# A new hand-written order for the first five units of a state-space scan feeding a squared-ReLU feed-forward, with w_in and w_out quarters issued earlier

## The chip, the cores and the metric

The kernel runs on one core of a Trainium2 chip. The metric is the device time of one execution in microseconds (us), less being better. The page of the profile shows one execution; its span runs from the first to the last instruction of the program.

The engines have short names in the profile. PE is TensorE, and PEld its weight loads. DVE (VectorE), ACT (ScalarE) and POOL (GpSimd) do the elementwise work. SP (SyncE) issues transfers, as ACT and POOL can.

## The reference

A chunked state-space scan over 4 batches and 8 heads, 768 positions, head width 32 and state width 16, is followed by a feed-forward with a squared ReLU.

```python
nc = S // 32
for c in range(nc):                        # xc, Bc, Cc: the chunk; state: [batch, H, 16, 32]
    cum = np.cumsum(log_a[:, :, sl], axis=-1)
    L = np.exp(cum[:, :, :, None] - cum[:, :, None, :]) * causal
    CB = np.einsum('bhin,bhjn->bhij', Cc, Bc)
    y_intra = np.einsum('bhij,bhjd->bhid', CB * L, xc)
    y_inter = np.einsum('bhin,bhnd->bhid', Cc, state) * np.exp(cum)[:, :, :, None]
    y[:, :, sl] = y_intra + y_inter
    state = decay_full * state + (sum over j of Bc[j] xc[j] * decay_from_j)
...
x = attn_out.transpose(0, 2, 1, 3).reshape(3072, 256)
h = np.maximum(x @ w_in, 0.0)              # w_in 256 x 2048
out = h * h @ w_out                        # w_out 2048 x 256
```

## The kernel before

The work is cut into twelve units. Unit k is 256 positions of one batch: units 0 to 3 are the first third of the four batches, 4 to 7 the second, 8 to 11 the last. Each unit goes through the scan and then, as a block of 256 tokens, through the feed-forward. The blocks have the letters a to l, in the order of the units.

The scan of a unit is done with prefix products P of the clipped a, so that the decay between two positions is a quotient. C is multiplied by P, x by the inverse of P, and the plain products of C and B are masked with the causal triangle.

**The order is a list.** The string `ORDER` is read word by word, and `one` (L655) calls the function of each word. The words run under a manual schedule: every engine does its instructions in the order in which the words issue them, and waits for its operands with semaphores. A last `:v`, `:a`, `:p` or `:s` names the engine (DVE, ACT, POOL, SP). The words that matter here, with k the unit:

- `fa0`, `fa1`, `la`: load a. The first two bring the pages of units 0 to 3 (a_nat, 64 rows, in halves), `la` the rest (128 rows).
- `ldBk`, `ldCk`, `ldxk`: load B, C or x of a unit (L125). `:l` and `:h` are the lower and upper four heads. `ldk` loads all three. `gB3` writes one element of unit 3's B tile on POOL, so that the load of that tile waits until POOL gets there.
- `wi0` to `wi3` and `wo0` to `wo3`: load a quarter of w_in (L139) or w_out (L143), issued by POOL.
- `sk`, `sn`: clip a and scan it; `sn` also multiplies `pick` by the totals. `sp`, `p`: turn the prefix products so that positions lie on partitions (L452). `iv`: their inverses (L546). `su`, `to`, `fq`, `pq`: totals and what is made of them.
- `jz`: clear a jt tile, which holds B and scaled C of a unit. `pbk`, `pck`: fill it with B (L170 or L168) and with C times P (L158). `pxk`: x times the inverse (xs, L177).
- `trk`: transpose jt, on PE (L195) for units 0 to 3 and by a transposing transfer on SP (L186) from unit 4; `tck` copies PE's result to bct (L208, L210).
- `mtk`: the products of C and B (L220). `mkk`: mask one of four quarters from PSUM on DVE (L229). `sck` and `msk`: copy a quarter with ACT (L234), then mask the copy (L238).
- `uk`, `ink` (or `inak`, `inbk`), `cak`: the state sums, the part inside the unit, the carried part, all on PE (L245). `tk` copies the result to T in bf16, `usk` the state sums; `sfk`, `zak`, `zbk`, `sak`, `sbk` form the next state.
- `rgk`: from unit 4 on, in one go, `ca` and `in` of unit k-1, the sums and `mt` of unit k.
- `a0` to `a7`: eight steps of the first feed-forward product of block a, four matmuls each (L403), and the ReLU on ACT (L408). `qa0`: the square on DVE (L414). `A0` to `A7`: four matmuls of the second product (L430); `A7` also copies the result out and stores it.
- `idn:c`: n dummy matmuls of c columns with ones (L476), which read no loaded data.
- `ti`, `pi`, `ku`, `ef`, `eb` make constants on POOL; `hd`, `pk`, `mb` and `wm` make others (heads and row sums on DVE, spread and pick_p on ACT, the causal mask on DVE, a first copy on ACT).

PSUM has eight banks. `bank` (L352) hands out the one used longest ago among those that are not held; two are for the second product's sums. A matmul into a bank waits until its last reader is done.

Of the kernel before, what the change touches and what calls it, by code (L numbers as in the profile page):

```python
# [30 lines left out]
def kernel(  # L31
# [32 lines left out]
        mk8 tr9 g5 qg4 G1 mk8 g6 qg5 G2 g7 qg6 G3 mk8 h0 qg7 G4 pc10 pb10 px10 ld11 h1 qh0 G5 mk8 h2 qh1 G6 h3 qh2
        G7 rg9 za9 zb9 sa9 sb9 h4 qh3 H0 mk9 tr10 h5 qh4 H1 mk9 h6 qh5 H2 h7 qh6 H3 mk9 i0 qh7 H4 pc11 pb11 px11
        i1 qi0 H5 mk9 i2 qi1 H6 i3 qi2 H7 rg10 za10 zb10 sa10 sb10 i4 qi3 I0 mk10 tr11 i5 qi4 I1 mk10 i6 qi5 I2 i7
        qi6 I3 mk10 j0 qi7 I4 j1 qj0 I5 mk10 j2 qj1 I6 j3 qj2 I7 rg11 za11 zb11 sa11 sb11 j4 qj3 J0 mk11 j5 qj4 J1
        mk11 j6 qj5 J2 j7 qj6 J3 mk11 k0 qj7 J4 k1 qk0 J5 mk11 k2 qk1 J6 k3 qk2 J7 rg12 k4 qk3 K0 k5 qk4 K1 k6 qk5
# [93 lines left out]

    def prep_b(k, eng, gs=(0, 1)):
        for g in gs:
            o = _fap(jt[k % 3], 16 * g, [[384, 2], [32, 4], [1, 16]])
            i = _fap(loaded[k]["B"], 128 * g, [[16, 2], [32, 4], [1, 16]])
            if eng is nc.scalar:
                eng.copy(out=o, in_=i)  # L168
            else:
                eng.tensor_copy(out=o, in_=i)  # L170
# [593 lines left out]
```

## Time and profile before

| | |
|---|---|
| median of 3 runs | 117.36 us (117.06 to 117.93) |
| profiled execution | 117.89 us, span 116.2 us |
| PE busy | 109.0 us (94%) |
| DVE busy | 85.0 us (73%) |
| ACT busy | 76.0 us (65%) |
| POOL busy | 49.3 us (42%) |
| transfers | 13.47 MB, mean 116 GB/s |
| PE's granted clock | full in all 40 slices |

Busy time is an engine's own instructions; issuing a transfer counts only on POOL. Rows of 40 digits are the span in 40 slices, each digit the busy share in tenths. q0 is the queue that POOL fills, q1 SP's, q10 ACT's. A transfer has two times: the issue on its engine, and the landing, when all of its data is there.

### The profile page before, as it was taken

The numbers are of one execution on the slowest core, as the hardware profiler recorded it, in microseconds if no ns is written. First come the engines' busy times: TensorE is split into PE (matmuls) and PEld (weight loads), VectorE is DVE, ScalarE is ACT, GpSimd is POOL, SyncE is SP. The second block draws the span as 40 slices with busy tenths as digits, with TensorE's granted clock in tenths as the row PEclk, the third lists the DMA queues.
The fourth block names the chain that finished last, engine by engine and source line by source line (L and its number), as shares of the span: only waits on it lengthen the run. The fifth ranks groups of instructions, "written<-read, shape, count | busy, mean of one in ns | idle before, by whom it ended". The sixth has DMA issues, their size and how long they took to land.

```text
span 116.2 us, 4109 instructions
## 1 busy us (share of the span) xinstructions
PE 109.0 (94%) x1677; PEld 97.0 (83%) x1677; DVE 85.0 (73%) x193; ACT 76.0 (65%) x155; POOL 49.3 (42%) x103
## 2 busy tenths in 40 slices
PE   7979898995999999999999999999999999999990
PEld 7856687784798988988989989989989899899980
DVE  1669986699595999988956989849758578445530
ACT  1455677454599656769475786687786776876840
POOL 6488860395348668566702569129020020000000
PEclk9999999999999999999999999999999999999999
DMA  1999999987888879936907818533033020020202
GB/s 35 200 174 186 189 201 201 222 151 138 164 51 184 184 154 230 159 73 166 172 6 182 159 55 174 118 101 63 3 117 50 0 93 6 0 90 0 96 0 90
DMA packets 47815, 13.47 MB, mean 116 GB/s; under 512 B 44276, under 2 KB 45876, under 8 KB 47796
## 3 DMA queue, kind: packets, MB, share of 16 engines
q1 hardware_dynamic: 44356, 10.77, 45.2%
q0 software_dynamic: 1664, 2.10, 11.2%
q10 hardware_dynamic: 1776, 0.34, 1.5%
q8 instruction: 13, 0.21, 0.8%
q14 instruction: 6, 0.05, 0.1%
HBM read 10.58 MB, written 3.15 MB: 118 GB/s over the span
## 4 chain that ended last, share of the span: by engine, by line
PE 77%; DMA 8%; DVE 5%; ACT 2%; issue 2%; POOL 2%; SPq 1%; ACTq 0%; POOLq 0%
PE pp L430 34%; PE pp L403 33%; PE pp L245 6%; DMA w_in_b<-in_moe_w_in_dram 6%; PE pp L220 3%; DMA B_nat<-in_B_dram 3%; DVE mts L229 2%; ACT hb L408 2%; DVE h L414 2%; POOL w_in_b L139 1%; DVE jt L170 1%; POOL jt L158 1%; POOL jt L170 0%; PE pp L195 0%; SPq L125 0%
## 5 line engine op out<-in xcount | busy, mean ns | idle before, releaser
L408 ACT ACTIVATE hb<-pp 128x512 bf16<-128x512 f32 x96 | 55.3, 598 | 26.5 <-PE pp L403 23.5
L403 PE MATMUL pp<-T,w_in_b 128*128 128x256 bf16 x384 | 54.6, 273 | 0.8 <-ACT bct L208 0.4
L430 PE MATMUL pp<-w_out_b,h 128*128 128x256 bf16 (+1 forms) x400 | 54.5, 268 | 0.0
L414 DVE TENSOR_TENSOR h<-hb 128x512 bf16<-128x512 bf16 x96 | 45.1, 489 | 12.6 <-ACT hb L408 12.3
L403 PEld LDWEIGHTS <-w_in_b 128*128 128x128 bf16 x384 | 41.2, 114 | 3.6 <-issue 1.7
L430 PEld LDWEIGHTS <-h 128*128 128x128 bf16 x400 | 37.5, 98 | 4.1 <-issue 0.6
L229 DVE TENSOR_TENSOR mts<-pp,mask 128x512 bf16<-128x512 f32 x45 | 29.9, 680 | 3.9 <-PE pp L220 3.7
L331 POOL TENSOR_TENSOR Sd<-z,Pquad 128x256 bf16<-128x256 f32 x16 | 10.6, 664 | 33.9 <-DVE z L315 24.4
L177 POOL TENSOR_TENSOR xs<-x_nat,Pinv 128x256 bf16<-128x256 f32 (+1 forms) x19 | 14.5, 781 | 3.3 <-DVE Pinv L546 1.4
L158 POOL TENSOR_TENSOR jt<-C_nat,P_sb 128x128 bf16<-128x128 f32 x22 | 9.5, 451 | 0.6 <-DMA C_nat<-in_C_dram 0.5
L476 PE MATMUL pp<-const-bfloat16-1.0 128*128 128x128 bf16 x73 | 6.9, 263 | 0.8 <-PEq L748 0.8
L315 DVE SCALAR_TENSOR_TENSOR z<-z,Ptot,us 128x64 f32<-128x64 f32 x8 | 2.3, 282 | 6.3 <-ACT us L299 6.3
L476 PEld LDWEIGHTS <-const-bfloat16-1.0 128*128 128x128 bf16 x73 | 6.1, 122 | 0.9 <-issue 0.8
L437 ACT COPY osb<-pp 128x512 f32<-128x512 f32 x11 | 6.4, 582 | 0.3 <-PE pp L430 0.3
L245 PE MATMUL pp<-mts,xs 64*32 64x128 bf16 x384 | 5.8, 219 | 0.0
L220 PE MATMUL pp<-bct 32*64 32x256 bf16 x192 | 5.4, 280 | 0.3 <-ACT bct L208 0.2
L170 POOL CAST jt<-B_nat 128x128 bf16<-128x128 f32 x18 | 5.0, 302 | 1.4 <-DMA B_nat<-in_B_dram 1.4
L245 PEld LDWEIGHTS <-xs 64*32 64x32 bf16 x384 | 4.0, 90 | 0.6 <-issue 0.4
L245 PE MATMUL pp<-bct,Sd 128*128 128x128 bf16 x40 | 4.2, 220 | 0.0
L195 PE MATMUL pp<-eye_b,jt 128*128 128x128 bf16 x24 | 2.0, 220 | 2.1 <-DVE jt L170 1.4
L282 ACT CAST T<-pp 128x512 bf16<-128x512 f32 x6 | 3.5, 586 | 0.4 <-PE pp L245 0.2
L208 ACT CAST T<-pp 128x256 bf16<-128x256 f32 x10 | 3.2, 376 | 0.7 <-PE pp L245 0.6
(63 smaller groups left out, 52.1 us busy)
## 6 DMA issues: line engine op xcount, KB each, us to landing
x_nat<-in_x_dram SPq DMA_DIRECT2D x11, 256.0 KB, 4.4
out_dram<-osb SPq DMA_DIRECT2D x11, 256.0 KB, 2.2
C_nat<-in_C_dram SPq DMA_DIRECT2D x11, 128.0 KB, 4.4
B_nat<-in_B_dram SPq DMA_DIRECT2D x11, 128.0 KB, 4.2
w_in_b<-in_moe_w_in_dram POOLq DMA_DIRECT2D x4, 256.0 KB, 7.0
w_out_b<-in_moe_w_out_dram POOLq DMA_DIRECT2D x4, 256.0 KB, 6.0
x_nat<-in_x_dram ACTq DMA_DIRECT2D x1, 128.0 KB, 3.8
x_nat<-in_x_dram SPq DMA_DIRECT2D x1, 128.0 KB, 4.1
```

Source lines behind the costliest of these rows:

```text
L158: eng.tensor_tensor(out=_fap(jt[k % 3], 128 + 144 * g, [[384, 2], [32, 4], [1, 16]]), in0=_fap(loaded[k]["C"], 128 * g, [[16, 2], [32, 4], ...
L177: eng.tensor_tensor(out=_fap(xs, 256 * r, [[256, 2 // n], [32, 8], [1, 32]]), in0=_fap(loaded[k]["x"], 32 * r, [[32, 2 // n], [64, 8], [1, ...
L220: nc.tensor.matmul(pp[64 * u:64 * u + 64, q, r * 256:r * 256 + 256], bct[32 * q:32 * q + 32, r, 0, u * 64:u * 64 + 64], _fap(bct[32 * q:32 ...
L229: nc.vector.tensor_tensor(out=live[k]["mts"][:, q].rearrange("p r g i -> p (r g i)"), in0=pp[:, q, :], in1=mask, op=ALU.mult)
L245: nc.tensor.matmul(dst, w, v, start=bool(need), stop=False, skip_group_check=True, **({} if pos is None else {"tile_position": pos}))
L331: nc.gpsimd.tensor_tensor(out=_fap(S_d, 0, [[128, 2], [32, 4], [1, 32]]), in0=_fap(z, 0, [[32, 2], [0, 4], [1, 32]]), in1=_fap(Pquad, 4 * ...
L403: nc.tensor.matmul(pp[:, h, i * 256:(i + 1) * 256], _fap(w, g * w.shape[2] + (o // 2) * 512 + 2 * (o % 2) + i, [[4, 128]]), T[blk][:, g].r ...
L408: nc.scalar.activation(out=hb.rearrange("p i t -> p (i t)"), in_=pp[:, h, :], func=AF.Relu)
L414: nc.vector.tensor_tensor(out=h2, in0=hb, in1=hb, op=ALU.mult)
L430: nc.tensor.matmul(dst, h2[:, i, r * 128:(r + 1) * 128], w_out_b[gi][:, 2 * o + i, c0:c1], start=first, stop=(fp == 7 and i == 1), skip_gr ...
L437: nc.scalar.copy(out=osb, in_=pp[:, 6 if blk == 1 else 7, :])
L476: nc.tensor.matmul(pp[:, h, 0:int(cols)], ones_b[:, 0:128], ones_b[:, 0:int(cols)] if dep is None else dep, start=True, stop=True, skip_gr ...
```

## The change

`ORDER` is written anew up to the fifth unit; from the word `tr6` on the two lists are the same. The parts that differ:

- **Order of loads.** On SP `la` stands first, then `fa0`, the lower halves of B0 and C0, C1, B1, both halves of x0 (one was on ACT's queue), x1 and the second unit's loads. On POOL wi0, wi1 and wo0 stand together ahead of `pb1` and `px0`; wi2 and wo1 follow ahead of `px1`. `gB3` moves up to the start.
- **Dummy matmuls.** 22 and 6 at the start in place of 12, 11 and 17; the later groups change a little (one has 256 columns).
- **Constants.** POOL makes eye_b, pick, quad and eye_f first and tri last. The second clip and scan come at the start; the clip is a word of its own (`ac`), for the second part of a on POOL, and the product with `pick` (`pp`) is ACT's.
- **Engines.** To POOL: the clearing of jt1, B of units 1 and 2, x of unit 0. To ACT: the causal mask, one half of T1, B of unit 3. To DVE: B of unit 0, C of unit 1, the mask of unit 0's copied quarter. Unit 2 has three quarters masked from PSUM and one copied by ACT and masked on DVE, where all four were masked from PSUM.
- **Merged copies.** `prep_b` without a half copies B of a unit in one instruction in place of two.
- **Feed-forward steps.** Blocks a to d come in another sequence among the words of units 2 to 4.

```diff
@@ ORDER, up to where the lists become one @@
-        id12:128 fa1:a ti pi ku id11:128 fa0:s id17:128 ldB0:h:a ldC0:h:a ldC0:l:s ldB0:l:s ef eb wm jz0:v hd
-        jz1:v jz2:v sk sp pc0:v pbl0:p id4:128 ldC1:s ldx0:l:s wi0 ldx0:h:a pk ldB1:s ps pbh0:p id1:128 iv1:0:8
-        trB0 trC0 tcB0:2:a tcC0:0:v tcC0:1:v ldx1:s px0:v id8:128 mt0 mb mk0 mk0 mk0 su id3:128 pc1:p u0:67 pb1:a
-        wi1 sc0 tr1 id8:128 to tc1:0:a tc1:1:a mt1 fq ms0:p sf0 wo0 iv:8:16 mk1 mk1 fr in0 sc1 ms1:v la ldB2:s ca0
-        px1:p wi2 gB3 t0:aa mk1 sn1 wo1 ldC2:s id9:128 a1 a0 u1 pc2 ina1 inb1 us0 a2 sf1 ca1 wi3 t1:vv pb2:v qa0
-        a3 p2 us1 b0 A0 qa3 qa1 b3 qb0 ldx2:s b1 b2 tr2 qb1 B0 tc2:0:a qb2 qb3 b4 b5 a5 A1 qa2 tc2:1:v zb1 zb0
-        ldC3:s qa5 ldB3:s A2 pq B3 mt2 qb5 B1 wo2 sb1 iv:16:32 px2 B2 mk2 sb0 mk2 mk2 A3 pc3 a6 b6 a4 wo3 mk2 u2
-        qa6 ldx3:s px3 qb4 pb3:v qa4 sf2 a7 b7 ld4 tr3 tc3:0:v A4 ca2 B4 us2 tc3:1:v ina2 inb2 u3:45 t2:aa A5 B5
-        us3 mt3 qb6 sc3 qa7 c1 pc4 c6 c0 qb7 za3 sa3 ld5 mk3 iv:32:64 ms3:v B6 pb4 qc1 mk3 qc0 tr4 px4 c5 qc5 zb3
-        B7 sb3 pb5 bk qc6 ld6 c2 px5 pc5 afC2 mk3 c4 A6 c3 tr5 A7 rg4 mk4 C0 qc4 za4 sa4 d3 d2 mk4 qc2 qd2 C6 c7
-        px6 qc3 qd3 pc6 C4 d1 C2 C1 C5 d0 qc7 ld7 mk4 mk4 C3 C7 qd0 zb4 rg5 sb4 D0 qd1 pb6 d4 tr6 mk5 za5 zb5 sa5
-        sb5 D1 iv:64:96 mk5 d5 qd4 D2 pb7 d6 qd5 d7 qd6 D3 zb2 e0 qd7 mk5 e1 qe0 sb2 D4 mk5 D5 ld8 pc7 e2 qe1 D6
...
+        eb pi id22:128 ku la fa0:s ef ac1:p fa1:a id6:128 ldB0:h:a ldC0:h:a jz1:p gB3 ti ldB0:l:s hd ac0:v sk0 wm
+        ldC0:l:s jz0:v sk1 pbl0:v pp1:a pbh0:v wi0 sp id3:256 trB0 pc0:v iv1:0:8 pk jz2:v wi1 ps ldC1:s ldB1:s
+        iv:8:16 tcB0:2:v ldx0:l:s id3:128 wo0 trC0 id4:128 tcC0:0:a mb:a pb1:p ldx0:h:s tcC0:1:v mt0 su pc1:v mk0
+        mk0 to id8:128 fr tr1 id10:128 mk0 sc0 id1:128 px0:p fq wi2 tc1:1:a u0:67 tc1:0:a mt1 ldx1:s ms0:v wo1 sf0
+        ldB2:s in0 sc1 ca0 id4:128 px1:p t0:aa id6:128 a0 a1 pb2:p mk1 ms1:v mk1 mk1 wi3 u1 ina1 inb1 sf1 ldC2:s
+        us0 p2 ca1 t1:va us1 a2 iv:16:32 qa1 a3 qa0 qa2 b0 b3 qb0 ldx2:s b1 b2 A0 zb0 iv:32:64 qb3 A1 B0 wo2 a5
+        pc2 sb0 qb1 qb2 qa3 b5 b4 qa5 qb4 a4 B1 tr2 tc2:1:a tc2:0:v A3 B2 ldC3:s qa4 mt2 B3 zb1 sc2 sb1 qb5 A2 px2
+        ldB3:s pq wo3 mk2 mk2 mk2 b6 a7 a6 pb3:a u2 ina2 ms2:v inb2 sf2 b7 pc3 B5 ldx3:s qb6 ca2 t2:aa us2 tr3 px3
+        tc3:1:v tc3:0:v B4 A4 mt3 u3:45 us3 qb7 A5 qa6 za3 qa7 ld4 sc3 c0 c6 ld5 sa3 pc4 c1 pb4 mk3 px4 mk3 mk3
+        tr4 qc0 pb5 c3 qc6 c7 px5 ld6 qc1 pc5 A6 qc3 ms3:v tr5 A7 B6 c5 qc5 c4 c2 C0 qc7 zb3 C6 sb3 qc4 C1 pc6 B7
+        C3 bk rg4 mk4 C5 ld7 za4 qc2 d2 C4 sa4 d0 d1 mk4 mk4 mk4 afC2 qd2 qd1 qd0 zb4 d3 px6 C2 C7 d4 rg5 sb4 pb6
+        D0 qd3 tr6 mk5 za5 zb5 sa5 sb5 D1 iv:64:96 mk5 d5 qd4 D2 pb7 d6 qd5 d7 qd6 D3 zb2 e0 qd7 mk5 e1 qe0 sb2 D4
...
@@ -149,25 +150,26 @@
 
     live = {}
 
-    def prep_c(k, eng, P=None, gs=(0, 1)):
+    def prep_c(k, eng, P=None):
         b, j = UNITS[k]
-        for g in gs:
-            p = P_sb if P is None else P
-            st = 96 if P is None else 32
-            col = (j * 32 if P is None else 0) + b * 8 + 4 * g
+        p = P_sb if P is None else P
+        st = 96 if P is None else 32
+        col = (j * 32 if P is None else 0) + b * 8
+        for g in range(2):
             eng.tensor_tensor(
                 out=_fap(jt[k % 3], 128 + 144 * g, [[384, 2], [32, 4], [1, 16]]),
                 in0=_fap(loaded[k]["C"], 128 * g, [[16, 2], [32, 4], [1, 16]]),
-                in1=_fap(p, col, [[st, 2], [1, 4], [0, 16]]), op=ALU.mult)
-
-    def prep_b(k, eng, gs=(0, 1)):
+                in1=_fap(p, col + 4 * g, [[st, 2], [1, 4], [0, 16]]), op=ALU.mult)
+
+    def prep_b(k, eng, gs=None):
+        fn = eng.copy if eng is nc.scalar else eng.tensor_copy
+        if gs is None:
+            fn(out=_fap(jt[k % 3], 0, [[384, 2], [16, 2], [32, 4], [1, 16]]),
+               in_=_fap(loaded[k]["B"], 0, [[16, 2], [128, 2], [32, 4], [1, 16]]))
+            return
         for g in gs:
-            o = _fap(jt[k % 3], 16 * g, [[384, 2], [32, 4], [1, 16]])
-            i = _fap(loaded[k]["B"], 128 * g, [[16, 2], [32, 4], [1, 16]])
-            if eng is nc.scalar:
-                eng.copy(out=o, in_=i)
-            else:
-                eng.tensor_copy(out=o, in_=i)
+            fn(out=_fap(jt[k % 3], 16 * g, [[384, 2], [32, 4], [1, 16]]),
+               in_=_fap(loaded[k]["B"], 128 * g, [[16, 2], [32, 4], [1, 16]]))
 
     def prep_x(k, eng):
...
         ones_f = nc.const_aps.tensor(1.0, [128, 128], FP32)
 
         def scan(m):
-            V.tensor_scalar(out=a_cl[m], in0=a_nat[m], scalar1=1e-6, scalar2=1.0, op0=ALU.max, op1=ALU.min)
             V.tensor_tensor_scan(out=cp[m], data0=a_cl[m],
                                  data1=nc.const_aps.tensor(0.0, [cp[m].shape[0], 128], FP32),
                                  initial=1.0, op0=ALU.mult, op1=ALU.add)
@@ -503,9 +504,15 @@
             keep_if(quad, ones_f[:, 0:4], [[-32, 4]], 0, 1)
             keep_if(quad, quad, [[32, 4]], 31, -1)
 
-        def causal():
-            V.tensor_copy(out=_fap(mask, 0, [[256, 2], [128, 2], [1, 128]]),
-                          in_=_fap(tri, 0, [[128, 2], [0, 2], [1, 128]]))
+        def causal(eng):
+            (A.copy if eng is A else eng.tensor_copy)(
+                out=_fap(mask, 0, [[256, 2], [128, 2], [1, 128]]), in_=_fap(tri, 0, [[128, 2], [0, 2], [1, 128]]))
+
+        def cleared(t, eng):
+            if eng is A:
+                A.copy(out=t.rearrange("p r w t -> p (r w t)"), in_=nc.const_aps.tensor(0.0, [128, 768], FP32))
+            else:
+                eng.memset(t, 0.0)
 
         def picked():
             A.copy(out=_fap(spread, 0, [[32, 4], [16, 2], [1, 16]]), in_=_fap(heads, 0, [[1, 4], [4, 2], [0, 16]]))
@@ -527,9 +534,14 @@
             P.tensor_tensor(out=Pquad[:, 0:8], in0=_fap(Ptot, 0, [[1, 8], [0, 4]]),
                             in1=_fap(quad, 0, [[0, 8], [1, 4]]), op=ALU.mult)
 
-        def second_scan():
-            scan(1)
-            V.tensor_scalar(out=pick_p[1], in0=pick, scalar1=cp[1][:, 127:128], scalar2=None, op0=ALU.mult)
+        def clamp(m, eng):
+            eng.tensor_scalar(out=a_cl[m], in0=a_nat[m], scalar1=1e-6, scalar2=1.0, op0=ALU.max, op1=ALU.min)
+
+        def second_pick(eng):
+            if eng is A:
+                A.activation(out=pick_p[1], in_=pick, func=AF.Copy, scale=cp[1][:, 127:128])
+            else:
+                V.tensor_scalar(out=pick_p[1], in0=pick, scalar1=cp[1][:, 127:128], scalar2=None, op0=ALU.mult)
 
         def second_p():
...
                 "wi": lambda: load_w_in(k), "wo": lambda: load_w_out(k),
                 "id": lambda: idle(k, f[1], dep(f[2]) if len(f) > 2 else None),
                 "ef": lambda: eye(eye_f, ones_f), "eb": lambda: eye(eye_b, ones_b[:, 0:128]), "wm": warmed, "hd": head_rows,
-                "jz": lambda: eng.memset(jt[k], 0.0), "ti": triangle, "pi": picks, "ku": quads,
-                "mb": causal, "pk": picked, "sk": lambda: scan(0), "sp": first_p, "sn": second_scan,
+                "jz": lambda: cleared(jt[k], eng), "ti": triangle, "pi": picks, "ku": quads,
+                "mb": lambda: causal(eng), "pk": picked, "ac": lambda: clamp(k, eng), "sk": lambda: scan(k), "sp": first_p, "pp": lambda: second_pick(eng),
                 "su": first_sums, "to": first_total, "fq": first_quad, "p": lambda: second_p(), "pq": second_quad,
                 "ps": lambda: A.copy(out=P_sb[:, :, 0:32], in_=P0.rearrange("p (r c) -> p r c", r=2)),
                 "iv": lambda: inv(int(f[1]), int(f[2]), k == 1),
```

More of the change, by code (lines that the diff above doesn't have):

```diff
@@ L59 @@
-        px6 qc3 qd3 pc6 C4 d1 C2 C1 C5 d0 qc7 ld7 mk4 mk4 C3 C7 qd0 zb4 rg5 sb4 D0 qd1 pb6 d4 tr6 mk5 za5 zb5 sa5
-        sb5 D1 iv:64:96 mk5 d5 qd4 D2 pb7 d6 qd5 d7 qd6 D3 zb2 e0 qd7 mk5 e1 qe0 sb2 D4 mk5 D5 ld8 pc7 e2 qe1 D6
-        e3 qe2 px7 D7 rg6 e4 qe3 za6 sa6 tr7 zb6 mk6 e5 qe4 sb6 e6 qe5 e7 qe6 mk6 E0 E1 E2 E3 ld9 px8 mk6 f0 qe7
-        E4 f1 qf0 pc8 E5 pb8 E6 mk6 f2 qf1 f3 qf2 E7 rg7 mk7 F0 f4 qf3 za7 tr8 F1 F2 f5 qf4 f6 qf5 f7 qf6 g0 qf7
-        zb7 sa7 sb7 mk7 F3 mk7 F4 pc9 pb9 px9 ld10 g1 qg0 F5 mk7 g2 qg1 F6 g3 qg2 F7 rg8 za8 zb8 sa8 sb8 g4 qg3 G0
@@ L64 @@
[L64 to L68, printed above, removed]
@@ L69 @@
-        K2 k7 qk6 K3 l0 qk7 K4 l1 ql0 K5 l2 ql1 K6 l3 ql2 K7 l4 ql3 L0 l5 ql4 L1 l6 ql5 L2 l7 ql6 L3 ql7"""
+        eb pi id22:128 ku la fa0:s ef ac1:p fa1:a id6:128 ldB0:h:a ldC0:h:a jz1:p gB3 ti ldB0:l:s hd ac0:v sk0 wm
+        ldC0:l:s jz0:v sk1 pbl0:v pp1:a pbh0:v wi0 sp id3:256 trB0 pc0:v iv1:0:8 pk jz2:v wi1 ps ldC1:s ldB1:s
+        iv:8:16 tcB0:2:v ldx0:l:s id3:128 wo0 trC0 id4:128 tcC0:0:a mb:a pb1:p ldx0:h:s tcC0:1:v mt0 su pc1:v mk0
+        mk0 to id8:128 fr tr1 id10:128 mk0 sc0 id1:128 px0:p fq wi2 tc1:1:a u0:67 tc1:0:a mt1 ldx1:s ms0:v wo1 sf0
@@ new lines @@
+        tr4 qc0 pb5 c3 qc6 c7 px5 ld6 qc1 pc5 A6 qc3 ms3:v tr5 A7 B6 c5 qc5 c4 c2 C0 qc7 zb3 C6 sb3 qc4 C1 pc6 B7
+        C3 bk rg4 mk4 C5 ld7 za4 qc2 d2 C4 sa4 d0 d1 mk4 mk4 mk4 afC2 qd2 qd1 qd0 zb4 d3 px6 C2 C7 d4 rg5 sb4 pb6
+        D0 qd3 tr6 mk5 za5 zb5 sa5 sb5 D1 iv:64:96 mk5 d5 qd4 D2 pb7 d6 qd5 d7 qd6 D3 zb2 e0 qd7 mk5 e1 qe0 sb2 D4
+        mk5 D5 ld8 pc7 e2 qe1 D6 e3 qe2 px7 D7 rg6 e4 qe3 za6 sa6 tr7 zb6 mk6 e5 qe4 sb6 e6 qe5 e7 qe6 mk6 E0 E1
+        E2 E3 ld9 px8 mk6 f0 qe7 E4 f1 qf0 pc8 E5 pb8 E6 mk6 f2 qf1 f3 qf2 E7 rg7 mk7 F0 f4 qf3 za7 tr8 F1 F2 f5
@@ new lines @@
+        qf4 f6 qf5 f7 qf6 g0 qf7 zb7 sa7 sb7 mk7 F3 mk7 F4 pc9 pb9 px9 ld10 g1 qg0 F5 mk7 g2 qg1 F6 g3 qg2 F7 rg8
+        za8 zb8 sa8 sb8 g4 qg3 G0 mk8 tr9 g5 qg4 G1 mk8 g6 qg5 G2 g7 qg6 G3 mk8 h0 qg7 G4 pc10 pb10 px10 ld11 h1
+        qh0 G5 mk8 h2 qh1 G6 h3 qh2 G7 rg9 za9 zb9 sa9 sb9 h4 qh3 H0 mk9 tr10 h5 qh4 H1 mk9 h6 qh5 H2 h7 qh6 H3
+        mk9 i0 qh7 H4 pc11 pb11 px11 i1 qi0 H5 mk9 i2 qi1 H6 i3 qi2 H7 rg10 za10 zb10 sa10 sb10 i4 qi3 I0 mk10
+        tr11 i5 qi4 I1 mk10 i6 qi5 I2 i7 qi6 I3 mk10 j0 qi7 I4 j1 qj0 I5 mk10 j2 qj1 I6 j3 qj2 I7 rg11 za11 zb11
@@ L70 @@
+        sa11 sb11 j4 qj3 J0 mk11 j5 qj4 J1 mk11 j6 qj5 J2 j7 qj6 J3 mk11 k0 qj7 J4 k1 qk0 J5 mk11 k2 qk1 J6 k3 qk2
+        J7 rg12 k4 qk3 K0 k5 qk4 K1 k6 qk5 K2 k7 qk6 K3 l0 qk7 K4 l1 ql0 K5 l2 ql1 K6 l3 ql2 K7 l4 ql3 L0 l5 ql4
+        L1 l6 ql5 L2 l7 ql6 L3 ql7"""
     WIN = [(0, 2), (2, 4), (4, 6), (6, 8)]
```

## The prediction

> **What bounds the kernel now.** I read the page first, then the chain in order of time, then busy time by stretch.
>
> ```profile
> PE 109.0 (94%) x1677; PEld 97.0 (83%) x1677; DVE 85.0 (73%) x193; ACT 76.0 (65%) x155; POOL 49.3 (42%) x103
> PE   7979898995999999999999999999999999999990
> DMA  1999999987888879936907818533033020020202
> ```
> ```profile
> 28.00:36.00 8.00, 8.00 (x132) 7.03 (x133) 6.59 (x17) 5.45 (x13) 3.33 (x7) 1.00 0.86 124
> 36.00:52.00 16.00, 16.00 (x319) 14.31 (x318) 14.38 (x31) 11.01 (x22) 11.36 (x24) 1.00 0.80 169
> ```
> In the stretches the columns are window, length, then PE, PEld, DVE, ACT and POOL. From 28 us PE is never idle, and the order of work is the same list in both kernels from `tr6` on. So only PE's lost time before that point can be won or lost: the 12.23 us until the first feed-forward matmul (L403), and the idle time until `tr3` at 27.93. The first 28 us of the DMA row are full as well. The chain says what ended last there:
>
> ```profile
> 7.46 6.58 DMA w_in_b<-in_moe_w_in_dram
> ...
> 18.04 1.08 ACT hb L408 x2
> ...
> 22.81 2.40 DVE mts L229 x4
> ...
> 25.54 1.63 DVE h L414
> 27.17 0.71 DVE jt L170 x2
> ```
> The second w_in quarter lands at 14.04; later ScalarE, then VectorE hold PE, last with unit 3's copy of B (`pb3:v`). Between 12.23 and 27.93 PE issued 64 matmuls of L403 and 32 of L430 (groups of that window). The chain has four at 0.44, so 96 x 0.109 = 10.5. From the same chain p2 takes 0.72 (L452 0.39, L537 0.33), tr2 0.35, mt2 0.35, u1 and u2 0.2, in1 0.45, ca1 0.11. That is 12.7 of 15.7 us: **3.0 us of idle time**, beside the 12.23.
>
> Which transfers get through in this stretch decides my forecast. Two looks at the queues, 12 to 14 us and 14 to 16 us (queue, kind: packets, MB, share of 16 engines):
>
> ```profile
> q0 software_dynamic: 246, 0.33, 110.2%
> q1 hardware_dynamic: 123, 0.02, 7.1%
> ```
> ```profile
> q1 hardware_dynamic: 1520, 0.31, 76.6%
> q0 software_dynamic: 82, 0.11, 37.3%
> ```
> q0 holds the weights that POOL issues, q1 SP's loads. Whenever q0 has packets, q1 almost stands still.
>
> **Part by part: the start, up to the first L403.** Twelve of the 40 opening dummy matmuls go (28 x 0.107 from 0.84 end at 3.8 us); the scan is ready by then, because `la` is now SP's first load and its clamp goes to POOL, VectorE no longer clears two jt tiles ahead of it, and POOL makes eye_f earlier: DVE waits 1.9 for it now. `pc0` needs C0's SP half, now SP's fourth issue instead of its second. Its neighbours set bounds: the B0 half issued at 1.73 took 3.1 (4.8), the whole C1 issued at 2.27 took 4.3 (6.6). I take 5.2, nearer the half of equal size. Then DVE in order: pc0 0.5, inverse 0.26, jt clear 0.38, inverse 0.24, two bct copies 0.58, pc1 0.48: 7.6. Three masks of unit 0 take 1.9 (as at 8.58): 9.5; `ms0`, now on DVE instead of POOL (1.14), 0.4: 9.9; Sd 0.41: 10.3. Beside it mt1 0.4 and ACT's score copy 0.6 end at 10.5, T 0.65 at 11.2. The first L403 goes at 11.25: **1.0 won**. If C0 lands at 6.6 it is 0.4 lost; at 4.8, 1.4 won.
>
> The new operations off that path: POOL's clamp (128x128) lies between its cast of that size, 0.29, and its largest product of that size, 0.62; POOL's clear of jt1 between a 0.12 memset and DVE's 0.38 doubled. I take 0.35 and 0.4, nearest the 128x128 cast; with four 0.29 selects for `tri`, POOL reaches wi0 at about 4.9 instead of 5.46. ACT's mask copy costs 0.59 (its 128x512 rows) ahead of 7.6, when the first mask product wants it; if ACT is late, all of it counts. ACT's pick product costs 0.3, DVE's second scan 0.42 and B0's two copies 0.35 while it waits for C0; all hidden, else 1.1. The merged B copy replaces two of 0.29: nothing either way. The gate `gB3` opens at 4 instead of 12.8 us, so B3 no longer waits for POOL; SP is behind its own backlog there anyway (the x2 issue occupies it from 7.58 to 11.46).
>
> **The weights ahead.** wi0, wi1 and wo0 are issued back to back: 0.90 + 0.77 + 0.60 from 4.9 to 7.2, where before they began at 5.46, 7.46 and 10.38. Behind them POOL does pb1 (0.5), px0 (1.05) and the first Pquad (0.23), then wi2 and wo1 to about 10.4 (before 12.05 and 12.84), and only then px1. All first uses of weights then lie behind their landings: wi1 at its old issue-to-landing of 6.6 is there at 12.4, while a2 asks at 14.
>
> The price is paid by q1. A quarter costs 11.2% of 116.2 us over eight, 1.63 us of all sixteen engines. In the old run x1 landed at 4.00 + 4.4 = 8.4. Now the weights begin to fill the engines at about 7.4, the load of a adds 0.15 ahead, and x0's second half moves from ACT's queue to SP's, ahead of x1. x0 just gets through; I leave 0.8 us of x1's 1.2 (1024 packets of 18.9 ns over 16) undone at 7.4. q1's share was 7.1% in the window above, 14.8% at 7.5 to 9.5, 47.7% over 7 to 15.6. With three quarters queued without a gap I take 20%, nearer to the lower ones: 4 us, so x1 lands at **11.4** (bounds 9.1 and 15.6). px1 takes 1.05 and 0.2 of handing on: u1 goes at 12.65. PE has ended a0 and a1 at 12.12: 0.53 idle. What is queued behind that wait: in1, p2, ca1 and every later matmul on PE; pb2 and wi3 behind px1 on POOL.
>
> **The trade until `tr3`.** After u1, PE has u1, in1, p2, ca1 (1.4), then 23 groups of four (10.05) and tr2, mt2, u2, in2, ca2 (1.36). New on other engines: unit 2 masks three quarters from PSUM (1.9) and one through ACT (0.4 on DVE), before four (2.4); pb2 (0.35) leaves DVE for POOL and pb3 (0.71) for ACT. ACT's relus come six in a row, 0.53 apart against PE's 0.44: 0.55 idle. I leave 0.3 for in2 and Sd behind DVE's masks. 12.65 + 1.4 + 10.05 + 1.36 + 0.85 = 26.3, and 0.5 more after it, since both copies of unit 3's bct (0.8) and a square (0.4) stand on DVE ahead of mt3 with only 0.87 of PE work over them: 26.8. The old order reaches the same work (B5, in2, ca2 added: 1.0) at 28.93. **Sum: 2.1 us won.** Later lists keep cover: `tr4` can go from SP at about 29, lands 2.8 later by the page's median for such transposes, and its user comes at 34.
>
> The profiled execution took 117.89 (span 116.2 and 1.7 around it), 0.5 above the median 117.36. I forecast 117.36 - 2.1 = **115.3**; a span of about 114.1.
>
> **Rivals.**
> 1. *x1 arrives in time* and the relus and masks keep up. For it: gaps like the 14 to 16 us one. Against: three quarters leave no gap. 0.53 + 0.85 more: 113.9. Chance 0.16.
> 2. *The weights shut out x1* (slower). q1 gets its 7%, and x1 lands when five quarters are through: 7.4 + 5 x 1.63 = 15.6. u1 goes at 16.85, 4.2 later than forecast; the 0.85 of later idle time hides behind it, leaving 3.35 against the 2.1 won: 118.6. It decides from a landing of x1 after 14.3. For it: the 12 to 14 us window, and px1 behind wi2 and wo1 in POOL's order, so that five quarters are under way. Against: the old q1 never stood still over 3 us. Chance 0.18.
> 3. *Turn by turn.* If the engines take one packet of each queue in turn, q1 gets 19 of every 144 ns: a q0 packet took 125 ns (11.2% of 16 x 116.2 us over 1664), a q1 packet 19 (45.2% over 44356). That is 13%; x1's 0.8 us takes 6.2 and lands at 13.6, u1 goes 2.2 later, 0.85 of it hidden: 116.6. For it: 14.8% at 7.5 to 9.5. Against: 76.6% and 7.1%. Chance 0.12. [...]
> 4. *The idle time only moves*: the middle keeps its 3.0 us, by bank or VectorE waits, in place of my 1.9: 116.4. For it: the old waits were ACT's and DVE's, and their work is nearly unchanged. Against: both B copies leave DVE. Chance 0.10.
> 5. *Half speed*: the opening dummies were 0.107 apart until 4.4 us, 0.058 after. [...] Chance 0.05.
>
> My forecast keeps 0.39, its own range 114.3 to 116.4. The range 113.7 to 118.7 takes in x1's two bounds and rivals 1 and 2. About 1% (1.2 us) is what a measurement tells from no change: faster has rival 1 and most of the forecast (0.52), slower rival 2 and some of the tails (0.26), the rest 0.22.
>
> **What would show it.** First L403 near 11.3; x1 landing near 11.4 and xs1 at once behind it; wi1 no longer in the chain; `tr3` near 26.3; PE full from 27; q1 under 25% of the engines from 7.5 to 11. The forecast is wrong if u1 goes after 14, if L403 starts after 12.2, or if DVE's masks or ACT's relus still own the chain from 22 to 27 us.

## The result, and the profile after

The new kernel takes 118.91 us (median of 20 executions, 117.57 to 123.88), the old one 117.34 (20, 116.74 to 118.52). The ratios here and below leave out executions over 1.5% above the fastest of their kernel, eight of the new one's twenty: by the ratio of 1.0071 (95% interval 1.0042 to 1.01) the change costs 0.4 to 1.0%, by the medians 1.3%, where 2.1 us were to be won. A repeat (e1_after below) gave 1.0165 (1.0062 to 1.0269).

The readings below are from the repeat's profiled execution, 118.50 us with a span of 116.8, which is 0.6 more than the old span. Its page, with the rows that stand against those shown of before, and the row of one more queue:

```profile
PE 108.9 (93%) x1671; PEld 97.5 (83%) x1671; DVE 83.4 (71%) x188; ACT 76.5 (65%) x157; POOL 49.5 (42%) x95
PE   7599829999999999999999999999999999999990
DMA  1999999989908995946906908623033020020202
q8 instruction: 13, 0.21, 0.8%
```

PE's busy time is the same (108.9 against 109.0). The holes of the old row in slices 7 and 10 have closed. In their place there is a 5 in the second slice and one digit 2: the sixth slice, 14.6 to 17.5 us. By stretch (window, length, PE, PEld, DVE, ACT, POOL), nothing is lost later, as before:

```profile
28.00:36.00 8.00, 8.00 (x147) 7.07 (x147) 7.33 (x16) 6.34 (x15) 5.81 (x11) 1.00 0.77 121
36.00:52.00 16.00, 16.00 (x263) 14.34 (x261) 14.04 (x32) 10.83 (x22) 11.24 (x21) 1.00 0.84 178
```

The chain that ended last, in order of time (start, length, what):

```profile
1.61 2.91 DMA a_nat<-in_a_dram
5.44 0.64 PE pp L454 x8
...
13.45 1.21 DVE mts L231 x2
15.05 2.02 issue
18.14 2.62 PE pp L405 x24
20.76 1.31 PE pp L432 x12
```

No wait for wi1 or for VectorE's copy of B is left in it: those old steps are gone, as forecast. In their place stands "issue": for 2.02 us PE waited for nothing that the profile shows. PE's own rows (start, length, operation; in brackets the idle time before and its releaser) place it:

```profile
13.15 1.06 PE L405 MATMUL pp<-T,w_in_b 128*128 128x256 bf16 x8 [0.32 <-DMA w_in_b<-in_moe_w_in_dram]
14.21 0.84 PE L247 MATMUL pp<-mts,xs 64*32 64x128 bf16 x28
17.07 0.24 PE L247 MATMUL pp<-mts,xs 64*32 64x128 bf16 x4 [2.02 <-issue]
29.62 0.50 PE L197 MATMUL pp<-eye_b,jt 128*128 128x128 bf16 x6
```

The stop falls inside one word, unit 1's `inb`, after 28 of its 32 equal matmuls. They read mts, whose last masks end at 14.66 (DVE's row of L231 there: 13.38 and 1.28 long), and xs of the unit, which `u1` had read before. So no operand was late. What else arrived then is in the queues (queue, kind: packets, MB, share of 16 engines). First the new kernel from 9 to 14.7 us, then from 14 to 15.5:

```profile
q0 software_dynamic: 591, 0.62, 86.0%
q1 hardware_dynamic: 1431, 0.19, 26.5%
```
```profile
q0 software_dynamic: 135, 0.22, 79.9%
q1 hardware_dynamic: 363, 0.07, 29.6%
q8 instruction: 1, 0.02, 3.7%
```

and the old kernel from 9 to 14.7 us:

```profile
q0 software_dynamic: 534, 0.62, 71.4%
q1 hardware_dynamic: 2731, 0.45, 45.3%
q8 instruction: 1, 0.02, 1.0%
```

q8 carries 13 transfers of 16 KB in either kernel. In the old one its first started at 10.38 us; in the new one it started at 14.76, and PE went on at 17.07. The theory to test: **these are PE's instructions**, and behind three weight quarters without a gap they came too late. In terms of the end, the old kernel's rows for the first feed-forward matmul and for `tr3` stand against those of the new one:

```profile
12.23 1.03 PE L403 MATMUL pp<-T,w_in_b 128*128 128x256 bf16 x8 [0.18 <-ACT T L208]
27.93 0.51 PE L195 MATMUL pp<-eye_b,jt 128*128 128x128 bf16 x6 [1.35 <-DVE jt L170]
```

The first L405 came 0.9 late (13.15 against 12.23), the stretch from there to `tr3` is 16.47 us against 15.70 + 1.0 of added work, 0.2 shorter although 2.0 of it is standing still; 0.9 - 0.2 = 0.7, and the span is 0.6 longer.

The first profile taken of the new kernel, of an execution of 121.76 us, has the same stop, longer. Its windows (the three numbers at the end are PE's granted clock, DMA share, GB/s):

```profile
16.00:18.00 2.00, 0.00 (x0) 0.00 (x0) 0.00 (x0) 0.00 (x0) 0.00 (x0) 1.00 1.21 208
18.00:20.00 2.00, 1.31 (x17) 1.18 (x18) 1.04 (x4) 0.11 (x2) 0.76 (x2) 0.82 1.23 203
20.00:22.00 2.00, 2.00 (x12) 1.38 (x11) 1.00 (x3) 1.46 (x6) 0.00 (x0) 0.50 1.20 209
```

From 16 to 18 us all five engines show no work, while the DMA engines move 208 GB/s. q8's first transfer started at 16.36, PE stood from 15.40 to 18.68, and then ran at a granted clock of 0.50 from 19.27 to 22.68 us.

### The profile page after: what moved, and what is told of

The parts are those of the page before. It is cut to its first block, busy times and chain, and to the rows that moved or that the text cites. A ratio compares the mean times of both kernels' runs of the same rounds, so it can differ in the third digit from the quotient of the medians.

```text
span 120.0 us, 4075 instructions
## 1 busy us (share of the span) xinstructions
PE 111.8 (93%) x1671; PEld 99.5 (83%) x1671; DVE 82.6 (69%) x188; ACT 76.8 (64%) x157; POOL 49.1 (41%) x95
## 4 chain that ended last, share of the span: by engine, by line
PE 90%; issue 3%; DMA 2%; DVE 1%; SPq 1%; ACT 0%; DVEq 0%; ACTq 0%
PE pp L405 37%; PE pp L432 35%; PE pp L247 7%; PE pp L477 4%; PE pp L222 3%; DMA a_nat<-in_a_dram 2%; PE pp L197 2%; PE pp L454 1%; SPq L565 1%; PE pp L549 0%; PE pp L528 0%; DVE Sd L345 0%; DVE cp L470 0%; ACT osl L734 0%; DVE a_cl L538 0%
## 5 line engine op out<-in xcount | busy, mean ns | idle before, releaser
L405 PE MATMUL pp<-T,w_in_b 128*128 128x256 bf16 x384 | 54.7, 278 | 0.0
L416 DVE TENSOR_TENSOR h<-hb 128x512 bf16<-128x512 bf16 x96 | 44.4, 482 | 13.6 <-ACT hb L410 13.5
L432 PE MATMUL pp<-w_out_b,h 128*128 128x256 bf16 (+1 forms) x400 | 53.8, 268 | 0.0
L405 PEld LDWEIGHTS <-w_in_b 128*128 128x128 bf16 x384 | 42.1, 115 | 2.9 <-issue 1.0
L231 DVE TENSOR_TENSOR mts<-pp,mask 128x512 bf16<-128x512 f32 x44 | 29.0, 680 | 3.6 <-PE pp L222 3.5
L179 POOL TENSOR_TENSOR xs<-x_nat,Pinv 128x256 bf16<-128x256 f32 (+1 forms) x20 | 16.0, 814 | 0.0
L159 POOL TENSOR_TENSOR jt<-C_nat,P_sb 128x128 bf16<-128x128 f32 x20 | 8.7, 454 | 3.9 <-DMA C_nat<-in_C_dram 3.9
L477 PE MATMUL pp<-const-bfloat16-1.0 128*128 128x128 bf16 (+1 forms) x67 | 8.3, 302 | 0.8 <-PEq L760 0.8
L345 DVE TENSOR_TENSOR Sd<-pp,Pquad 128x256 bf16<-128x256 f32 x3 | 1.3, 424 | 5.9 <-PE pp L247 5.9
L167 POOL CAST jt<-B_nat 128x256 bf16<-128x256 f32 x10 | 4.3, 434 | 0.0
L236 ACT CAST sc<-pp 128x512 bf16<-128x512 f32 x4 | 2.4, 588 | 1.9 <-PE pp L222 1.9
```

The lines of the kernel that those rows point to most:

```text
L159: eng.tensor_tensor(out=_fap(jt[k % 3], 128 + 144 * g, [[384, 2], [32, 4], [1, 16]]), in0=_fap(loaded[k]["C"], 128 * g, [[16, 2], [32, 4], ...
L179: eng.tensor_tensor(out=_fap(xs, 256 * r, [[256, 2 // n], [32, 8], [1, 32]]), in0=_fap(loaded[k]["x"], 32 * r, [[32, 2 // n], [64, 8], [1, ...
L231: nc.vector.tensor_tensor(out=live[k]["mts"][:, q].rearrange("p r g i -> p (r g i)"), in0=pp[:, q, :], in1=mask, op=ALU.mult)
L405: nc.tensor.matmul(pp[:, h, i * 256:(i + 1) * 256], _fap(w, g * w.shape[2] + (o // 2) * 512 + 2 * (o % 2) + i, [[4, 128]]), T[blk][:, g].r ...
L416: nc.vector.tensor_tensor(out=h2, in0=hb, in1=hb, op=ALU.mult)
L432: nc.tensor.matmul(dst, h2[:, i, r * 128:(r + 1) * 128], w_out_b[gi][:, 2 * o + i, c0:c1], start=first, stop=(fp == 7 and i == 1), skip_gr ...
```

## The experiments

The rival to the theory of late instructions was the forecast's own: some data (x1, a weight quarter, a state) is late, and the label "issue" hides it. A second rival was the clock: only 28 opening dummies leave PE at half speed for longer, and everything behind it shifts. (The trace's clock records begin, at full, at 4.52 us in the old kernel, at 9.03 in the repeat and at 12.44 in the first profile. The page's clock row shows full ahead of them too, but the repeat's dummies were 0.107 us apart until 8 us and 0.060 from 9.3.) The first five runs set these against each other.

**e1_after**: the new kernel unchanged.

> The changed kernel as it is, for a second execution with its own trace. The first one stood still on TensorE from 15.40 to 18.68 us inside in1 (L247), with no semaphore named, and the one 16 KB transfer on the instruction queue q8 that TensorE needs next ran only at 16.36 us, where before it ran at 10.38. Theory F (the weights shut out TensorE's own instruction transfer): the wait is there in this execution too whenever the first q8 transfer comes after about 14 us, and at the same matmul; its length follows the time of that transfer, so times from 117.5 to 122. Theory X (x1 or C2 is late): the wait moves with the landing of a load and no q8 transfer goes with it. Theory S (the start is late and cold): first L405 near 13.9 whatever q8 does, worth about 1.6 us against 12.23.

119.49 us (118.50 to 121.30, 4), ratio 1.0165 (of two of them). The stop is there again, at the same matmul. Up to it PE had issued 223 matmuls and 223 weight loads in this record, and 223 and 223 in the first one, though that stop began 0.35 us later. A place that is fixed by a count, and not by a time, speaks for instructions. And in both PE went on with its 224th matmul 2.3 us after q8's first transfer started (14.76 to 17.07, 16.36 to 18.68).

**e2_warm**: twelve more opening dummies, as many as the old list has.

```diff
-id22:128
+id34:128
```

> The changed kernel with 34 instead of 22 opening dummy matmuls, so 40 in all before sp, as the kernel before has them. Theory S: TensorE reaches full clock near 4.5 us instead of 12.4, the dummies of 8 and 10 cost 0.5 us less each, the first L405 comes at 13.0 or sooner, 0.9 us or more faster than the changed kernel wherever that has no q8 wait. Theory F: the 24 added instructions make TensorE ask for the next block sooner, near 9.5 us; the wait in in1 gets shorter or goes, since the weights begin only at 8.5 us. If neither the clock nor the order of q8 matters: within 0.3 us of the changed kernel.

116.35 us (115.97 to 116.47, 4), ratio 0.9893 (0.9847 to 0.9939). Twelve dummies of ones turn a loss into a gain of 1%. PE's rows:

```profile
13.34 1.06 PE L405 MATMUL pp<-T,w_in_b 128*128 128x256 bf16 x8 [0.56 <-DMA w_in_b<-in_moe_w_in_dram]
14.40 0.83 PE L247 MATMUL pp<-mts,xs 64*32 64x128 bf16 x32
27.55 0.50 PE L197 MATMUL pp<-eye_b,jt 128*128 128x128 bf16 x6
```

The first L405 is no earlier than in e1_after; `in1` runs through its 32 matmuls, and `tr3` comes 2.07 earlier, just the stop. q8 had its turn at 10.42, under weights that fill the engines, 10 to 11 us:

```profile
q0 software_dynamic: 147, 0.15, 100.1%
q1 hardware_dynamic: 154, 0.02, 16.5%
q8 instruction: 1, 0.02, 5.9%
```

So a transfer of instructions did get through beside weights here, with q0 at 100.1%. But the twelve dummies made PE warm sooner (full clock from 4.66, against 9.03 in the repeat) and also moved every later instruction 24 places on. e5 and e6 part these.

**e3_gap**: the burst of weights is undone, all else stays.

```diff
-jz2:v wi1 ps
+jz2:v ps
-id3:128 wo0 trC0
+id3:128 trC0
-fq wi2
+fq wi1 wo0 wi2
```

> The changed kernel with wi1 and wo0 issued by GpSimd after the first Pquad (ahead of wi2) instead of behind wi0. Theory F: with only wi0 under way until about 12 us the first q8 transfer runs near 11 us, TensorE does not stand still in in1, and the times lose their spread: 117.5 at most, 1 us or more under the changed kernel's median. Theory X or S alone: the first L405 stays near 13.9 and the time stays at 118 or gets worse by wi1, which now lands near 16 and is wanted at 15.5.

117.47 us (116.84 to 118.45, 10), ratio 0.9999 (0.9965 to 1.0034). No wait for instructions; q8's first transfer started at 13.18, not near 11 as expected. It was only just in time: PE too was late (first L405 at 13.74, and half clock from 8.06 to 11.47) and reached its 224th matmul at 15.42, 2.2 us after that start. wi1, now later, made `a2`, the third step of the block, wait 0.54. Without the burst this kernel neither loses nor wins.

**e4_burst**: the old kernel with wi1 and wo0 directly behind wi0.

```diff
-wi0
+wi0 wi1 wo0
```
(and the old places of `wi1` and `wo0` left out)

> The kernel before with one part of the change alone: wi1 and wo0 issued directly behind wi0. Theory F: q0 is busy without a gap from 7.5 to 12.5 us, the q8 transfer that ran at 10.38 is put off to 12.5 or later, and TensorE, which runs out of instructions near 13.5, stands still for 0 to 3 us in some executions; time 117.3 to 120, spread over more than 1 us. Theory S (only the start and the clock cost time): no wait, wi1 lands sooner than 14.04, time 117.1 or 0.2 us faster than before. Theory X: la, B2 and C2 land later, xs1 is not touched since x1 landed at 8.4 already, no change.

119.82 us (119.27 to 120.90, 4), ratio 1.0205 (1.0136 to 1.0274), and no wait for instructions: the expectation missed. The loss has another way in. On POOL `pbh0` now stood behind two more weight issues, the transpose of unit 0's B went at 7.89 instead of 6.73, PE ran at half clock from 8.69 to 15.51, and the first L403 came at 14.54. q8's first transfer did come late, at 14.06, but PE reached its 224th matmul only at 16.29, 2.2 us after it. As a test of the theory this run says little; as a price for issuing weights on POOL ahead of its own work it says 2%.

**e5_wide**: meant to be as warm as e2, but with the instruction count of the new kernel (four dummies of 512 columns in place of sixteen).

```diff
-id22:128
+id18:128 id4:512
```

> The changed kernel with its first 22 dummy matmuls made longer, not more: 18 of 128 columns and 4 of 512, so that TensorE is busy until about 5.1 us, as with 40 of 128, while the number of its instructions stays that of the changed kernel. Clock theory: all of what 12 more dummies won (3.1 us by the medians 119.49 and 116.35) came from reaching full clock at 4.7 us; this kernel then takes 116.3 too. Count theory: it came from asking for the instruction block 24 instructions sooner, ahead of the weights; this kernel then has full clock near 4.7, but its first q8 transfer at 13 us or later and a wait of TensorE inside in1, 117.5 to 119. Both: in between, with a wait of under 1 us.

Median 119.99 us (117.31 to 121.36, 10), above the 117.5 to 119 expected; ratio 1.0023 (0.9981 to 1.0066, of four of them). The profiled execution, the fastest of the ten, took 117.31:

```profile
14.37 0.76 PE L247 MATMUL pp<-mts,xs 64*32 64x128 bf16 x28
15.91 0.24 PE L247 MATMUL pp<-mts,xs 64*32 64x128 bf16 x4 [0.78 <-issue]
```

Warm (full clock from 5.56), with the same first L405 as e2 (13.30), and still a stop, at the same matmul, after 223 and 223 again. The clock alone doesn't take it away. It is shorter than in e1_after, with q8 at 13.48 instead of 14.76; PE went on 2.4 us after that.

**e6_count**: the other half: twelve more instructions, but no more dummy columns (24 dummies of 64 for 12 of 128).

```diff
-id22:128
+id10:128 id24:64
```

> The changed kernel with the same dummy time and 12 more dummy instructions: 10 of 128 columns and 24 of 64 in place of 22 of 128. Count theory: TensorE asks for its block 24 instructions sooner, the first q8 transfer runs at 12 us or sooner, there is no wait in in1, and the time is 1 to 2 us under the changed kernel's 119.49, with the clock full only at 8 to 12 us as there. Clock theory: nothing changes but the count, so the wait in in1 stays and the time stays at 118 to 120.

116.45 us (116.09 to 117.45, 8), ratio 0.9912 (0.9873 to 0.9952); that is 3.0 under the 119.49, more than the 1 to 2 expected. PE got its full clock only at 10.09, and the first L405 came later than in any other run of the new list. Yet:

```profile
14.23 1.06 PE L405 MATMUL pp<-T,w_in_b 128*128 128x256 bf16 x8 [0.99 <-DMA w_in_b<-in_moe_w_in_dram]
15.29 0.57 PE L247 MATMUL pp<-mts,xs 64*32 64x128 bf16 x32
```

No stop; q8 came at 12.00, 3.5 us before PE's 224th matmul (15.47). The count decides, not the warmth and not the data: e5 and e6, each with one trace, settle it between the theory and both rivals.

**e7_ti**: e2 with POOL's triangle moved ahead of `ac1`, where POOL only waits for a, so that wi0 goes as early as the prediction had it.

```diff
-id22:128
+id34:128
-ef ac1:p
+ef ti ac1:p
```
(and the old place of `ti` left out)

> The kernel with 12 more dummies and the four selects of tri (1.2 us of GpSimd) moved ahead of the clip of a, into GpSimd's 1.8 us wait for a. With 12 more dummies alone the first L405 waited until wi0 landed at 13.29, T being ready at 12.69, and pb1 and px0 stood behind three weight issues on GpSimd. If GpSimd's late start holds the feed-forward back: wi0 is issued near 5.7 instead of 6.86, pb1 and px0 are done 1.1 us sooner, the first L405 comes near 12.3 and the time is 0.5 to 1 us under the 116.35 of 12 more dummies alone. If weights that start at 7.9 instead of 9.0 us get in the way of x1 (landed 9.55 there): x1 lands at 11 to 13, u1 waits for xs1 and the time is 116.4 or more. If they get in the way of the q8 transfer: a wait in in1 as in the changed kernel, 117.5 or more.

117.31 us (115.58 to 118.61, 4), ratio 0.9886 (0.9787 to 0.9986, of two of them). wi0 was issued at 5.81 instead of 6.90, the first L405 went at 12.03, and then the forecast's own next step came true:

```profile
13.58 0.25 PE L247 MATMUL pp<-xs,jt 64*32 64x64 bf16 x16 [0.52 <-POOL xs L179]
```

x1 landed at 12.35, 6.5 us after its issue, where in e1_after it landed at 9.51; u1 waited 0.52, and the block of instructions was 0.35 late once more (q8 at 12.08, PE on at 14.40). PE stopped at 223 and 223 again: with twelve dummies more, that is now after 16 of the 32 matmuls of `inb`, twelve earlier. The earlier start of the weights was paid for at both, with 0.52 and 0.35 us.

**e8_many**: the count driven further: 74 dummies of 64 columns in place of 22 of 128.

```diff
-id22:128
+id74:64
```

> The changed kernel with 74 dummy matmuls of 64 columns in place of 22 of 128: TensorE is busy until about 5.1 us, and 104 instructions are added ahead of sp. Count theory: the block that TensorE asks for near its 165th instruction is then asked for near 5.5 us, 3 us before the weights begin; its q8 transfer runs at 8 us or sooner, there is no wait in in1 in any execution, and the time is that of 12 more dummies, 116.0 to 116.5, with no execution over 117. If each dummy instruction has a price of its own beyond its columns, sp comes later than 5.2 and the time is 116.5 to 118.

116.16 us (115.57 to 116.57, 4), ratio 0.9873 (0.9815 to 0.993). q8's first transfer started at 6.36, after 181 recorded PE instructions and before any weight; no stop; the first L405 at 12.64. PE next waited 0.38 for wi1.

**e9_wi0**: e8 with wi0 ahead of `ti` on POOL.

```diff
-gB3 ti
+gB3 wi0 ti
```
(and the old place of `wi0` left out)

> The same, and wi0 issued ahead of the four selects of tri, wi1 and wo0 as before behind them. If the first L405 waits for wi0 alone (with 12 more dummies T was ready at 12.69 and wi0 at 13.29): wi0 is issued near 5.7 and lands near 12, the first L405 goes at 12.7, x1 lands by 11, and the time is 0.3 to 0.7 us under the kernel with 74 dummies, 115.5 to 116. If a weight that starts near 7.7 us shuts out x1, as the run with tri moved showed (x1 at 12.35): u1 comes after 13.9 and nothing is won.

116.31 us (115.48 to 116.49, 4), ratio 0.9876 (0.982 to 0.9932): nothing over e8, and above the 115.5 to 116 expected. wi0, issued at 5.69, landed at 12.27, but the first L405 went at 13.34, 0.7 later than in e8: now x was late, x0's second half (10.02, with `px0` at 10.19) and x1 (11.72).

**e10_before_many** and **e11_before_few**: the old kernel with 80 dummies of 64 columns for its 40 of 128, and with 10 of 512. If many dummies help by themselves, the first must gain; if a late transfer on q8 is enough for a stop, the second must lose.

```diff
-id12:128 ... id11:128 ... id17:128
+id24:64 ... id22:64 ... id34:64
```
```diff
-id12:128 ... id11:128 ... id17:128
+id3:512 ... id3:512 ... id4:512
```

> The kernel before with its 40 opening dummies of 128 columns made 80 of 64, the same TensorE time. Count theory: its first q8 transfer moves from 10.38 to 8 us or sooner, but it never stood still for instructions, so the time stays: 117.2 to 117.7. If more instructions ahead help of themselves (by the clock or otherwise), it is 0.5 us or more faster here too.

> The kernel before with its 40 opening dummies of 128 columns made 10 of 512: the same TensorE time, 60 instructions fewer, and the list of loads untouched. Count theory: the block that TensorE asks for near its 165th instruction is asked for near 9 us, after the weights have begun (7.3 to 8.3), its q8 transfer runs at 12 to 15 instead of 10.38, and TensorE stands still before its 450th instruction: 0.5 to 3 us lost, 117.8 to 120. If the wait belongs to the new list alone (three weight quarters in a row), nothing changes: 117.2 to 117.7.

117.20 us (116.89 to 118.41, 10), ratio 0.9981 (0.9948 to 1.0015), and 117.42 (116.76 to 118.16, 10), ratio 0.9997 (0.9966 to 1.0028). The first is as expected. The second missed its wait. q8's first transfer did start later, at 12.49 instead of 10.38. But with 60 instructions fewer ahead of it PE's 224th matmul came later too, at 16.02 instead of 13.50, and 3.5 us lay between the two. A late transfer alone was no stop. In the four traces with a stop it began between 0.96 us before q8's start (first profile) and 1.97 us after it (e7); in the late transfers without one its 224th went 2.2 us (e3, e4) to 3.5 us (e6, e11) after it.

**e12_many_again**: e8 once more with more rounds, since it beats both kernels.

> The kernel with 74 dummies of 64 columns once more, in more rounds, for the size of what the change wins when TensorE's instruction block is there: a ratio of 0.985 to 0.992 to the kernel before, with no execution as slow as 118. If the four executions of the first time were luck, the ratio comes above 0.995.

116.17 us (115.54 to 119.04, 11) against 117.44 of the old kernel: ratio 0.9884 (0.985 to 0.9918, of eight of them). Two of the eleven took 118.20 and 119.04, where none as slow as 118 was expected; no profile shows such an execution, and its cause is open. The profiled one took 115.75, span 114.0, and its chain begins:

```profile
0.81 3.28 DMA a_nat<-in_a_dram
4.17 0.65 POOL a_cl L538
4.87 0.74 POOL jt L515
...
7.62 7.46 DMA w_in_b<-in_moe_w_in_dram
15.13 2.81 PE pp L405 x24
```

POOL's work ahead of the weights and wi1's landing hold the end now.

## Why the prediction was wrong, point by point

**What bounds the kernel.** Right: only PE's lost time before `tr3` counted; from 28 us on both kernels are full.

**The start: wrong, and all its 1.0 us.** It failed at its first sentence, "the scan is ready by then, because `la` is now SP's first load". The a of units 0 to 3 comes with `fa0` and `fa1`, and `fa0` now stands behind the 64 KB of `la`: it landed at 4.5 instead of 2.40, and the first transposes (`sp`) went at 5.44, where the old kernel had them at 5.14. Nothing was won that the later steps could hand on. DVE shows what it cost (rows of the repeat):

```profile
4.62 0.22 DVE L538 TENSOR_SCALAR a_cl<-a_nat 64x128 f32<-64x128 f32 x1 [1.95 <-DMA a_nat<-in_a_dram]
5.33 0.38 DVE L515 MEMSET jt<- 128x384 uint32 x1
5.63 0.35 DVE L470 TENSOR_TENSOR_SCAN cp<-a_cl,const-float32-0.0 128x128 f32<-128x128 f32 x1
5.91 0.53 DVE L171 CAST jt<-B_nat 128x128 bf16<-128x128 f32 x2
6.37 0.47 DVE L159 TENSOR_TENSOR jt<-C_nat,pp 128x128 bf16<-128x128 f32 x2
```

C0's half landed at 5.32, as forecast (5.2), but `pc0`, the last row, went only at 6.37. With a so late, the clearing of jt0, the second scan and B0's copies no longer fitted in front of C0's landing: the forecast had the scan and the copies as "all hidden, else 1.1", and they were not hidden. From `pc0` to T it took 6.4 us, against 6.0 forecast. POOL's terms were mis-sized too:

```profile
4.40 0.65 POOL L538 TENSOR_SCALAR a_cl<-a_nat 128x128 f32<-128x128 f32 x1 [2.14 <-DMA a_nat<-in_a_dram]
5.10 0.74 POOL L515 MEMSET jt<- 128x768 bf16 x1
5.83 1.12 POOL L481 TENSOR_SCALAR_AFFINE_SELECT tri<-const-bfloat16-1.0 64x128 bf16<-64x128 bf16 x4
6.90 1.68 POOL L140 DMA_DIRECT2D w_in_b<-in_moe_w_in_dram  x2
8.58 0.57 POOL L144 DMA_DIRECT2D w_out_b<-in_moe_w_out_dram  x1
9.19 0.39 POOL L167 CAST jt<-B_nat 128x256 bf16<-128x256 f32 x1
```

The clamp took 0.65 (taken as 0.35, between bounds of 0.29 and 0.62), the clear 0.74 (0.4), and I had left out the wait of 2.14 for `la` in front of them. wi0 went at 6.9, not 4.9, landed at 13.11, and held the first L405 until 13.15; T was ready at 12.75 (ACT's copy), against a forecast of 11.2. The forecast's own sign of being wrong, a first L403 after 12.2, came true. Rival 5 (half speed) named the right danger: in the repeat full clock came at 9.03, before the first L405, but in the first profile, with PE at half clock until 12.44, T was ready only at 13.80 and the first L405 went at 13.85.

**x1 behind the weights: the mechanism is right, and it didn't decide.** Three quarters back to back did hold q1 down: 17.5% of the engines from 12 to 14 us in the repeat, where I took 20%. ("Whenever q0 has packets, q1 almost stands still" was too strong: the second of the two looks beside it has q1 at 76.6% next to q0's 37.3%.) But the weights began to fill the engines near 9.1, not 7.4, so x1 was through (9.51, forecast 11.4). With the weights at 7.5 (e7) it landed at 12.35, within a microsecond of the forecast, and u1 waited 0.52. That the forecast had 0.53 is partly luck: x1 and the end of `a1` both came about 0.9 later than forecast. In the repeat the loads that starved were unit 2's C (7.4 to 19.0 us) and x (8.3 to 23.5), off the path.

**Until `tr3`: right in sign, too small.** Forecast: 11.25 to 26.3 and 0.5 more, 15.55 us, against 16.7 of the old kernel, 1.1 won. Without the stop it is 14.21 (e2) or 14.17 (e12, 12.63 to 26.80), 2.5 won. ReLUs, masks and the copies of B kept up; the 1.9 us of idle time that I left there was not needed, though the work itself took 14.2 us and not 13.7.

**What was missing: PE's instructions.** No rival has them, though the page of before has the row "q8 instruction: 13, 0.21, 0.8%", and its first transfer of 0.02 MB lies in the very stretch whose queues I read. Rival 2 ("the weights shut out x1") had the right culprit and the wrong victim; that its 118.6 lies near the measured time is luck, as x1 was not late. Sums: without the stop, 1.1 are lost at the start (e2's 13.34) and 2.5 won behind it, 1.4 in all; the spans say 116.2 - 114.7 = 1.5. With it, 2.0 are given back, and the kernel is slower. Against the forecast span of 114.1 the repeat's 116.8 is 2.7 longer: the start 1.9 worse than forecast, 2.0 of standing still, less 1.1 by which the rest was better.

**How far the mechanism is shown.** The stop was at the same recorded instruction, 223 matmuls and 223 weight loads, in four traces with different times (stops from 14.0 to 15.4 us) and in three kernels with different dummies, in one of them another matmul of `inb`; it ended in each case 2.3 to 2.4 us after q8's first transfer started; it went when twelve dummies were added and no time (e6), and stayed when time was added and no instructions (e5). That q8 carries PE's instructions shows in its later transfers as well: the thirteenth starts after 3229 to 3245 recorded matmuls and weight loads in all fourteen traces, at times from 100.9 to 112.6 us, though the kernels have 3294 to 3446 of them. From e11 to e10, which differ in PE's dummies alone, it moves from 109.98 to 103.33.

What asks for the first block, and at which instruction, no row shows (the "165th" of some expectations was an estimate of mine). Nor is it shown what makes the new kernel's longest executions long: all eight over 119.5 us have a mean granted clock of 0.955 to 0.986, nine of the other twelve have 1.00, so lost clock goes with them, but only one of the eight has a trace.

q8's transfers are of 16 KB each. From the fourth to the thirteenth they started on average 254 recorded matmuls and weight loads apart in the repeat and in the first profile, 253 in the old kernel. The stop of 2.02 us came after 446 recorded ones, with no transfer on q8 before 14.76.

## What to carry to other kernels

Read the row of the instruction queue on the page, and where large transfers are issued without a gap, ask when the next block of instructions has to come through them: "issue" ahead of PE in the middle of a run of equal matmuls was the sign here (2.02 us after 28 of 32). If it shows, try a gap in the burst (e3: no stop, ratio 0.9999) or let the engine get on with its instruction stream before the burst starts: here the new list with 52 more, shorter dummies is 1.2% faster than the old kernel (e12). And when a load is moved to the front of a queue, cost what it moves back: here the start term was lost from the 64 KB load on (`fa0` landed at 4.5 instead of 2.40 us).

## What was new of the hardware

- PE's instructions came as transfers of 16 KB on q8, beside the data. The first started between 6.24 us (e12) and 16.36 us (first profile of the new kernel, with q0 at 80.5% of the engines from 9 to 16.3 us), and in four traces PE stood still for 0.35 to 3.29 us.
- A stop of 3.29 us was followed by a granted clock of 0.50 from 19.27 to 22.68 us; after a stop of 2.02 us it stayed at 1.00. The fall came 0.6 us after PE had gone on (18.68).
- Dummies of 64 columns ran 0.053 us apart before the clock was full (e12, until 4.18 us), those of 128 columns 0.107: twice the instructions in the same time.
- A transfer of instructions did not help at once: in four traces PE went on 2.3 to 2.4 us after q8's first transfer started, though the transfer itself took only 0.9 to 1.0.
- The weights' median from issue to landing was longer with the burst: w_out quarters took 6.0 us in the old kernel and 8.5 in the repeat.
